# The first phase of an S4D and attention kernel, recorded and put in order by a list scheduler

## The chip, the cores and the metric

One core of one Trainium2 chip. The metric is the device time of one execution in microseconds (us); lower is better. All arithmetic is float32 (the matmuls read their operands as float32r, a float32 format of the matrix engine, and so work on high and low parts). The engines are TensorE (PE), VectorE (DVE), ScalarE (ACT), GpSimd (POOL) and SyncE (SP), whose queue issues nearly all DMA transfers.

## The reference

Two independent layers on 2048 positions of width 448, joined along the last axis:

```python
def _A_ref(u, log_A_real, A_imag, C_real, C_imag, log_dt, D_skip):
    dt = jnp.exp(log_dt)
    A = -jnp.exp(log_A_real) + 1j * A_imag
    C = (C_real + 1j * C_imag) * dt[:, None]
    P = jnp.exp((A * dt[:, None])[:, :, None] * pos[None, None, :])
    K = 2.0 * jnp.einsum("dn,dnl->dl", C, P).real       # 256 states, 2048 positions
    y = irfft(rfft(u_t, 2 * L) * rfft(K, 2 * L))[..., :L]
    return y.transpose + u * D_skip

def _B_ref(x, wqkv, wo):
    q, k, v = heads(x @ wqkv)                            # 16 heads of 28
    p = softmax(q @ k.T * 28 ** -0.5)
    return merge(p @ v) @ wo

out = concatenate([A, B], axis=-1)
```

## The kernel before

The kernel has a first phase and a main loop.

**The first phase** does two things side by side. One is the projections of attention. The input is taken in four chunks of 512 rows. A chunk is transposed on PE (`transposes`, tiles `xn`, `pt`, then `xh` and `xl`, its high and low parts), and then multiplied by the weights in 12 jobs: a key and a query job for each of four groups of four heads (`qk_proj`), and four value jobs of 128 rows (`v_proj`). That makes 48 jobs, each of 12 matmuls of up to 512 columns into one PSUM tile `pm` (three in rotation). A job's eviction writes its result as high and low part into one of two `hl` tiles (ACT, then DVE), and SP stores it to DRAM (`k`, `q`). Key jobs of the first two chunks also make differences of keys (`kb`, `dhl`, stored as `kd`, loaded again as `kdif`). Value results go through two `v` tiles.

The other is the seeds of the S4D layer: eight groups (`seeds(o)`), each a chain of 13 stages over ACT, DVE, POOL and PE. Parameters are loaded (`nat`), scaled by `dt`, transposed into PSUM (`pn`), turned into phases and sizes (`tri`, 1680 columns), through sines and exponentials on ACT (each needs its own function table, loaded on a change), multiplied on POOL and DVE, and stored as `sd` from two tiles: `se`, which shares its memory with the query tiles `qhat`, and `sg`.

Behind both come the maxima of the first unit. A unit is one group of heads with one chunk of queries. The softmax of the main loop subtracts a bound on each row, made ahead of it: 16 groups (four heads, four blocks of 128 queries) of five matmuls each against the keys `khat`, the key differences `kdif` and the negated queries `nq`, a Relu on ACT and one instruction on DVE that adds and takes the maximum. For the first unit:

```python
pd, pb = (ps_2.tile([128, 2, CQ], F32, name="p2") for _ in range(2))
kb = kt.rearrange("p (c s n) -> p c s n", c=NQ, s=2)[:, :2, 1, :]
mm(pd[:, 0], q, kd_g[0, j], start=True, stop=True)
mm(pd[:, 1], q, kt[:, 2 * CQ:3 * CQ], start=True, stop=False)
mm(pd[:, 1], nq[:, j, ts], kt[:, 3 * CQ:], start=False, stop=True)
mm(pb[:, 0].rearrange("p (c n) -> p c n", c=2), q, kb, start=True, stop=True)
mm(pb[:, 1], q, kt[:, 3 * CQ:], start=True, stop=True)
nc.scalar.activation(rl, pd, AF.Relu)
nc.vector.tensor_tensor_reduce(rl, pb, rl, 1.0, -3.0e38, ALU.add, ALU.max, m_u[0, 1][:, i:i + 1])
```

The 16 bounds of a row block are transposed (`max_end`) and written as two rows into the query tile by DMA (`max_put`), and only then can the first score matmul run (`pss<-qhat,khat`).

**What sets the order.** The phase is written as a loop over 41 steps (lines 517 to 530) that deals out projection jobs, seed stages (a new group every four steps) and loads. In this phase the entry of `KEPT` (line 88) is empty: the framework's own scheduler may reorder the instructions of each engine by its own estimates and priorities, and its result is what the profile shows. In the main loop (`KEPT["a"]`) each engine keeps the order of the program.

Two places in memory tie the order. The weights of the queries and keys lie in the tile that later takes the keys of the first group (`w_g` in `k0_t`, line 233), so a head's keys can be loaded only when the weights there are done. And in the last chunk the value jobs come first. The loads of the keys, 4 heads of 4 transfers, are asked for at steps 33, 35, 36 and 37 (`KW`, `load_k`), those of the key differences and first queries at steps 26 to 35.

**The main loop** runs over 16 units of 16 key blocks: scores, exponentials, products with the values, the next unit's maxima, and between them the S4D layer in small pieces (powers of the seeds, matmuls, Fourier steps). Its first instructions read the first unit's keys, queries, bounds, the values and the first seeds (`sdb<-sd`).

Of the kernel before, what the change touches and what calls it, by code (L numbers as in the profile page):

```python
# [8 lines left out]
F32 = mybir.dt.float32  # L9
F32R = mybir.dt.float32r  # L10
# [7 lines left out]
L = 2048  # L18
# [25 lines left out]
A0, A1, KW = 26, 34, (33, 35, 36)  # L44
# [21 lines left out]
class Kept:  # L66
# [5 lines left out]
    def __getattr__(self, name):  # L72
        f = getattr(self.engine, name)

        def call(*args, **kw):
            i = f(*args, **kw)  # L76
            return self.owner.tc.keep_in_program_order(i) if self.name in self.owner.kept else i
        return call


class Engines:
    def __init__(self, tc):
        self.tc, self.kept = tc, ()
# [8 lines left out]
def body(ctx, tc, a, out):  # L92
# [41 lines left out]
    k0_p = pool(k0_st, "k0_p", side="right")  # L134
    k0_t = k0_p.tile([128, HG, L], F32R, name="khat")
# [10 lines left out]
    def load_k(g, j, p):  # L146
        if j == 0:
            t = k0_t if g == 0 else p.tile([128, HG, L], F32R, name="khat")
# [50 lines left out]
    def max_end(u, ps):  # L199
        nc.tensor.transpose(ps[:16, :128], m_u[u, 1], ident)  # L200
        mh = q_p.tile([16, 2, 128], F32R, name="mh")
# [11 lines left out]
    with ExitStack() as st:  # L213
        sst, xst, wst, mst, psx, psm = (ExitStack() for _ in range(6))
# [3 lines left out]
        y_p = pool(wst, "y_p", side="right")  # L218
        ps_w[0] = pool(psx, "ps_w", 1, PSUM)
# [3 lines left out]

        xns = {}

        def load_x(c):
            xs = x[c * CQ:(c + 1) * CQ, :].rearrange("(t p) d -> p t d", p=128)
            for h in range(2):
                xns[c, h] = y_p.tile([128, 2, D], F32, name="xn", bufs=3)
# [6 lines left out]
        nc.gpsimd.memset(k0_t[:CK].rearrange("p g (n e) -> p (g n) e", e=32)[:, :, DH:].bitcast(F32), 0.0)  # L236
        vst = [v_p.tile([128, NK // NQ, HG, 32], F32, name="v", bufs=5).rearrange("p t h e -> p (t h) e") for _ in range(2)]
        for t in vst:
            nc.gpsimd.memset(t[:, :, DH:DH + 1], 1.0)
            nc.gpsimd.memset(t[:, :, DH + 1:], 0.0)  # L240
        wns = []
        for i in range(2):
            wn = t_p.tile([128, 3, LV, BO * 16], F32, name="tri", bufs=2).rearrange("p t k h -> p (t k h)")
            wn = wn[:CK, :2 * 3 * D].rearrange("p (k s d) -> p k s d", k=2, s=3)
            wns += [wn[:, 0], wn[:, 1]]
# [7 lines left out]
        def load_nat(o):  # L253
            nats[o] = s_p.tile([PO, 4, 256], F32, name="nat", bufs=2)
# [50 lines left out]
        def turn_dt():  # L305
            dt_ps = ps_t.tile([128, CQ], F32, name="pt")[:PO, :NO]
# [7 lines left out]
        def seeds(o):  # L314
# [13 lines left out]
            def turn():  # L328
                pn = ps_n.tile([128, CQ], F32, name="pn")
# [6 lines left out]
                q["tr"] = s_p.tile([128, NH], F32, name="tr", bufs=2)  # L336
                act.activation(q["tr"], ps[:, 0].rearrange("p b h e -> p (b h e)"), AF.Copy)

            def phases():
                tri = t_p.tile([128, 3, LV, NH], F32, name="tri", bufs=2)  # L340
# [14 lines left out]
            def places():  # L355
                se = q_p.tile([128, HG, CQ], F32R, name="qhat", bufs=3).bitcast(F32).rearrange("p h q -> p (h q)")
# [5 lines left out]
            def g_place():  # L362
                q["sg"] = sg = s_p.tile([128, BO, SDF - F_G], F32, name="sg", bufs=SGB)
# [36 lines left out]
            def g_first():  # L400

                c0 = q["ps"][:, 2:4].rearrange("p c b h e -> p c (b h e)")
                px = ps_x.tile([128, CQ], F32, name="px")
# [29 lines left out]
        def transposes(c):  # L433
            for k in range(NCK):
                pt = ps_t.tile([128, CQ], F32, name="pt")[:CK]
                for t in range(4):
                    nc.tensor.transpose(pt[:, t * 128:(t + 1) * 128], xns[c, t // 2][:, t % 2, k * CK:(k + 1) * CK], ident)
                xh[k] = x_p.tile([CK, CQ], F32R, name="xh", bufs=XB)
                xl[k] = x_p.tile([CK, CQ], F32R, name="xl", bufs=XL)
# [3 lines left out]
        def qk_proj(c, s, g):  # L443
            pp = w_tile()
# [7 lines left out]
            def evac():  # L452
                hl = x_p.tile([128, 2, CQ], F32R, name="hl", bufs=2)
# [7 lines left out]
                if s == 1 and c < 2:  # L461
                    HC = CQ // 2
                    kb = y_p.tile([128, HC], F32, name="kb")
                    dhl = y_p.tile([128, 2, HC], F32R, name="dhl")
# [10 lines left out]
        def v_proj(c, t):  # L475
            pp = w_tile()
# [12 lines left out]

        work = []  # L490
# [15 lines left out]
        pend, n_work = [], len(work)  # L506
# [7 lines left out]
        for j, t in enumerate(KW):  # L514
            ahead[t].append(lambda j=j: load_k(0, j, k0_p))

        def project():

            e = work.pop(0)() if work else None
            while pend:  # L520
                pend.pop(0)()
            if e:
                pend.append(e)

        for t in range(n_stage):
            while work and n_work - len(work) < n_work * (t + 1) / PW:
                project()
            for f in slots[t] + ahead.get(t, []):
                f()
            if t + 1 == PW:  # L530
                project()
                wst.close()
                load_k(0, HG - 1, k0_p)
                load_q(1)
                for c in range(NQ):
                    load_v(0, c)
        xst.close()
        psx.close()
        m_p = pool(mst, "m_p")
        ps_2 = pool(psm, "ps_2", 4, PSUM)  # L540
        nq = m_p.tile([128, HG, CQ], F32R, name="nq")
        m_u[0, 1] = q_p.tile([128, HG * 4], F32, name="m1", bufs=2)
        for i in range(16):
            j, t = divmod(i, 4)
            ts = slice(t * 128, (t + 1) * 128)
            q, kt = q_u[0][:, j, ts], kt_g[0][j]
            if t == 0:
                nc.gpsimd.tensor_scalar(nq[:, j], q_u[0][:, j].bitcast(F32), -1.0, None, op0=ALU.mult)
            pd, pb = (ps_2.tile([128, 2, CQ], F32, name="p2") for _ in range(2))
            kb = kt.rearrange("p (c s n) -> p c s n", c=NQ, s=2)[:, :2, 1, :]  # L550
            mm = nc.tensor.matmul
            mm(pd[:, 0], q, kd_g[0, j], start=True, stop=True)
            mm(pd[:, 1], q, kt[:, 2 * CQ:3 * CQ], start=True, stop=False)
            mm(pd[:, 1], nq[:, j, ts], kt[:, 3 * CQ:], start=False, stop=True)
            mm(pb[:, 0].rearrange("p (c n) -> p c n", c=2), q, kb, start=True, stop=True)
            mm(pb[:, 1], q, kt[:, 3 * CQ:], start=True, stop=True)
            rl = m_p.tile([128, 2, CQ], F32, name="rl2", bufs=2)
            nc.scalar.activation(rl, pd, AF.Relu)
            nc.vector.tensor_tensor_reduce(rl, pb, rl, 1.0, -3.0e38, ALU.add, ALU.max, m_u[0, 1][:, i:i + 1])
        nc.scalar.activation(half_pi[:1], half_pi[:1], AF.Exp)  # L560
        max_end(0, ps_2.tile([128, 2, CQ], F32, name="p2")[:, 0])
        max_put(0)
        psm.close()
        mst.close()
# [12 lines left out]
    k_pools = [k0_p, kq_p]  # L577
# [580 lines left out]
```

## Time and profile before

| | |
|---|---|
| median of three runs | 1304.7 us (1302.42 to 1306.85) |
| profiled execution, its own time | 1307.74 us |
| its span, first to last instruction | 1305.7 us |
| mean granted clock of TensorE | 0.976 |
| busy: PE, ACT, DVE, POOL | 94%, 75%, 69%, 66% of the span |

In a row of the profile stand the line of the kernel, the engine, the operation, the tile written and the tiles read, shapes and types. All engine calls go through one helper, so the line of nearly every instruction is that helper's call (L76 before the change, L80 or the recorder's call after it); instructions are told apart by their tiles. `p<-khat,qhat` (tile `p2`, its number left out) are the first unit's maxima, `pm<-xh,khat` and `pm<-xl,khat` are projections, because the weights lie in the tile named `khat`. `[2.18 <-DMA qhat<-mh]` behind a row means that the engine was idle for 2.18 us before it and what it waited for. SPq and ACTq are the queues in which DMAs are issued. In a table by stages, a stretch from:to in us is followed by its length, each engine's busy time and instruction count, the granted clock of PE, the busy share of the DMA engines and GB/s.

### The profile page before, as it was taken

The page shows a single profiled execution, that of the slowest core. Times are in us where ns is not written, and L with a number is a line of the kernel's source. Part 1 is how long each engine was busy: PE and PEld are TensorE (multiplying, and loading weights), DVE is VectorE, ACT ScalarE, POOL GpSimd, SP SyncE. Part 2 cuts the span into 40 slices and gives each one's busy share as a digit, 9 for nine tenths or more (in the row PEclk, how much of TensorE's full clock was granted, in tenths as well). Part 3 has the DMA queues.
Part 4 walks back from the last instruction along what each step waited for, and adds up shares of the span by engine and source line. Part 5 has one row for each costly group of instructions (what it writes and reads, how often), then busy time and mean ns, then how long its engine had stood idle before and what let it go on. Part 6 is the DMA issues. An engine that isn't in the chain of part 4 may idle for free.

```text
span 1305.7 us, 32148 instructions
## 1 busy us (share of the span) xinstructions
PE 1228.7 (94%) x12193; PEld 695.7 (53%) x12193; DVE 907.0 (69%) x2001; ACT 980.3 (75%) x2046; POOL 865.9 (66%) x684
## 2 busy tenths in 40 slices
PE   6888877799999999999999999999997999999998
PEld 5766755355555555555555555555554555545333
DVE  5676656677777787777788888888986555636111
ACT  4877875588888888888788888888886666756463
POOL 2677654478888788888769999999995221424421
PEclk9989887799999999999999999999999999999999
DMA  6677679735866455468634232743324453647666
GB/s 202 207 273 257 218 259 271 212 66 136 185 147 142 109 149 157 142 169 231 162 104 105 56 83 62 157 111 78 82 59 139 146 158 136 203 142 238 202 161 175
DMA packets 200082, 205.28 MB, mean 157 GB/s; under 512 B 95992, under 2 KB 158520, under 8 KB 197880
## 3 DMA queue, kind: packets, MB, share of 16 engines
q1 hardware_dynamic: 199864, 203.22, 56.1%
q8 instruction: 96, 1.57, 0.5%
q14 instruction: 58, 0.48, 0.1%
q10 hardware_dynamic: 64, 0.02, 0.0%
HBM read 120.74 MB, written 82.18 MB: 155 GB/s over the span
## 4 chain that ended last, share of the span: by engine, by line
PE 72%; POOL 8%; ACT 7%; DVE 5%; DMA 4%; issue 4%; SPq 0%; ACTq 0%; POOLq 0%
PE pm L76 39%; PE pss L76 16%; PE po L76 16%; POOL sg L76 2%; POOL e L76 2%; DMA khat<-k 2%; POOL tri L76 2%; ACT tri L76 1%; ACT sg L76 1%; DVE mx L76 1%; POOL p L76 1%; ACT L76 1%; ACT p L76 1%; POOL eu L76 1%; DVE rl L76 1%
## 5 line engine op out<-in xcount | busy, mean ns | idle before, releaser
L76 ACT ACTIVATE p<-pss 128x512 f32<-128x512 f32 x1024 | 560.4, 609 | 109.9 <-PE pss L76 105.9
L76 PE MATMUL pss<-qhat,khat 128*128 128x512 f32 x1024 | 405.7, 402 | 4.0 <-DMA qhat<-mh 2.2
L76 DVE TENSOR_REDUCE mx<-pm 128x1 f32<-128x512 f32 x480 | 308.3, 683 | 121.2 <-PE pm L76 119.5
L76 PE MATMUL pm<-khat,qhat 128*128 128x512 f32 x720 | 314.4, 437 | 6.1 <-ACT rl L76 3.5
L76 POOL TENSOR_TENSOR e<-e,sdb 128x256 f32<-128x256 f32 x168 | 202.0, 1203 | 108.7 <-ACT e L76 67.2
L76 PE MATMUL po<-p,v 128*32 128x512 f32 x2048 | 271.0, 597 | 0.0
L76 POOL TENSOR_TENSOR e<-e,eu 128x256 f32<-128x256 f32 x168 | 248.3, 1478 | 13.2
L76 PEld LDWEIGHTS pm<-khat,qhat 128*128 128x128 f32 x720 | 135.4, 188 | 206.4 <-ACT p L76 47.0
L76 PEld LDWEIGHTS pss<-qhat,khat 128*128 128x128 f32 x1024 | 191.2, 189 | 52.5 <-ACT p L76 13.8
L76 DVE CUSTOM_DVE_ANT_0 rl<-pm,rl 128x512 f32<-128x512 f32 x240 | 165.3, 689 | 70.0 <-ACT rl L76 67.7
L76 POOL TENSOR_TENSOR eu<-e,sdb 128x256 f32<-128x256 f32 x168 | 202.3, 1204 | 0.0
L76 POOL TENSOR_TENSOR p<-pr,pr 64x448 f32<-64x448 f32 x64 | 73.2, 1144 | 155.6 <-PE pm L76 122.3
L76 DVE TENSOR_TENSOR g<-g,zg 128x128 f32<-128x128 f32 x392 | 162.0, 413 | 3.6
L76 ACT ACTIVATE rl<-pm 128x512 f32<-128x512 f32 x240 | 145.3, 605 | 7.7 <-issue 4.1
L76 PE MATMUL pm<-xh,khat 112*128 112x512 f32 x256 | 89.7, 431 | 19.6 <-DVE hl L76 10.6
L76 PE MATMUL pm<-kdif,qhat 128*128 128x512 f32 x240 | 97.0, 404 | 1.7 <-DVE pr L76 1.1
L76 DVE TENSOR_TENSOR zg<-g,zg 128x128 f32<-128x128 f32 x224 | 88.0, 393 | 5.3
L76 PEld LDWEIGHTS pm<-e,g 128*32 128x32 f32 x3584 | 56.9, 110 | 49.2 <-issue 15.7
L76 PE MATMUL pm<-e,g 128*32 128x64 f32 x3584 | 73.6, 223 | 8.7 <-POOL e L76 8.7
L76 ACT ACTIVATE y<-pm 128x448 f32<-128x448 f32 x48 | 26.5, 553 | 59.7 <-PE pm L76 39.1
L76 PEld LDWEIGHTS pm<-xh,khat 112*128 112x128 f32 x256 | 51.0, 205 | 35.9 <-DVE hl L76 12.6
L76 DVE TENSOR_TENSOR pr<-pm,ub 128x448 f32<-128x448 f32 x64 | 37.0, 619 | 46.9 <-PE pm L76 37.7
(133 smaller groups left out, 1491.6 us busy)
## 6 DMA issues: line engine op xcount, KB each, us to landing
sdb<-sd SPq DMA_DIRECT2D x56, 336.0 KB
khat<-k SPq DMA_DIRECT2D x64, 256.0 KB
qhat<-q SPq DMA_DIRECT2D x64, 256.0 KB
sd<-sg SPq DMA_DIRECT2D x8, 1456.0 KB
k<-hl SPq DMA_DIRECT2D x16, 512.0 KB
q<-hl SPq DMA_DIRECT2D x16, 512.0 KB
v<-v SPq DMA_DIRECT2D x32, 256.0 KB
mw<-in_mw SPq DMA_DIRECT2D x16, 512.0 KB
```

What stands on the lines that cost most here:

```text
L76: i = f(*args, **kw)
```

## The change

The first phase is no longer handed to the framework in the order written. Each engine call is recorded (`Plan.add`) with its tiles and byte ranges, from which follows what each waits for (`link`). At the end `order` walks through all recorded operations with set durations, and picks at each step, for the engine that is free first, the ready operation with the longest remaining chain; the calls are then made in that order and each engine keeps it (`KEPT["p"]` names all five engines).

For this, tiles are taken in fixed rotation (`ring`) in place of pools that hand out slots. The weights get a tile of their own, `w`. Three of the four `xl` tiles lie in memory of the value tiles `v`. The first group's keys get a tile in the memory that the input tiles, the value weights `vh` and `vl`, and `kb` and `dhl` leave (`change`); they are asked for after jobs 41 to 44, the third and fourth head's first. In the last chunk the first group's key job goes ahead of the value jobs. The 16 groups of maxima are recorded from job 43 on, each in two halves of 512 columns, with two Relus and two maxima, into PSUM tiles of the projections and transposes (`pt`, `pm`); a last reduction joins the halves. Loads of the differences and first queries are asked for at steps 18 to 29 of the loop.

```diff
-A0, A1, KW = 26, 34, (33, 35, 36)
+A0, A1 = 18, 28
+MG = {41: (2, ()), 42: (3, ()), 43: (0, (8, 9)), 44: (1, (10, 11)), 45: (None, (12, 13)), 46: (None, (14, 15)), 47: (None, (0, 1)),
+      48: (None, (2, 3)), 49: (None, (4, 5)), 50: (None, (6, 7))}
...
+            if self.owner.plan is not None:
+                return self.owner.plan.add(self.name, name, f, args, kw)
...
+class Plan:
+    SPANS = {("gpsimd", "tensor_tensor", 784): 1.87, ("gpsimd", "tensor_tensor", 672): 1.73, ("gpsimd", "tensor_tensor", 1680): 3.0,
...
+             ("gpsimd", "tensor_scalar", 672): 2.28, ("gpsimd", "tensor_scalar", 512): 1.49, ("vector", "tensor_tensor", 1680): 2.3}
+    SCALE = {"p": 1.0, "s": 1.6, "m": 1.0, "d": 1.0}
+    BIAS = {"p": 0.0, "s": -20.0, "m": 0.0, "d": 0.0}
+    GAP, TABLE = 0.06, 1.28
...
+            o.span = self.SPANS.get((engine, method, n)) or {
+                "scalar": 0.2 + 0.00083 * n + (0 if tight else 0.1), "vector": 0.15 + 0.00104 * n + (0 if tight else 0.16),
+                "gpsimd": 0.2 + (0.0 if method == "memset" else 0.0025) * n}[engine]
...
+    def order(self):
...
+        for o in reversed(self.ops):
+            k = o.tag, o.engine
+            tail[o.i] = max([cost(o) + self.GAP + tail[j] for j in after[o.i]] + [o.span + chain.get(k, 0.0), cost(o)])
+            chain[k] = tail[o.i] if o.engine != "sync" else 0.0
...
+        while len(out) < n:
+            e = min((e for e in pools if pools[e]), key=lambda e: max(free[e], min(ready[i] for i in pools[e])))
+            t = max(free[e], min(ready[i] for i in pools[e]))
+            best = max((i for i in pools[e] if ready[i] <= t + 1e-9),
+                       key=lambda i: tail[i] * self.SCALE[self.ops[i].tag] + self.BIAS[self.ops[i].tag] - (0 if self.ops[i].table in (None, table[0]) else self.SWITCH))
...
-KEPT = {"p": (), "a": ("tensor", "vector", "scalar", "gpsimd", "sync"), "f": ()}
+KEPT = {"p": ("tensor", "vector", "scalar", "gpsimd", "sync"), "a": ("tensor", "vector", "scalar", "gpsimd", "sync"), "f": ()}
...
-        w_g = k0_t[:CK].rearrange("p g (i s k h e) -> p i s k g h e", i=2, s=2, k=NCK, h=HG)
+        w_t = w_p.tile([CK, HG, L], F32R, name="w")
+        w_g = w_t.rearrange("p g (i s k h e) -> p i s k g h e", i=2, s=2, k=NCK, h=HG)
...
+        def change():
+            yst.close()
+            k0.append(pool(k0_st, "k0_p", side="right"))
+            t = k0[0].tile([128, HG, L], F32R, name="khat")
+            kt_g[0] = [t[:, i] for i in range(HG)]
...
+                nc.gpsimd.tensor_scalar(Late(("nq", j), CQ, lambda: nqs[j]), q_u[0][:, j].bitcast(F32), -1.0, None, op0=ALU.mult)
...
+            for h in range(2):
+                pd, pb = pt_r(), pm_r()
+                if h == 0:
+                    mm(pd, q, kd_g[0, j], start=True, stop=True)
+                    mm(pb.rearrange("p (c n) -> p c n", c=2), q,
+                       k_late(j, CQ, lambda t_: t_.rearrange("p (c s n) -> p c s n", c=NQ, s=2)[:, :2, 1, :]), start=True, stop=True)
+                else:
+                    mm(pd, q, quarter(2), start=True, stop=False)
+                    mm(pd, Late(("nq", j), 128, lambda: nqs[j][:, ts]), quarter(3), start=False, stop=True)
+                    mm(pb, q, quarter(3), start=True, stop=True)
+                rl = rl_r()
+                nc.scalar.activation(rl, pd, AF.Relu)
+                nc.vector.tensor_tensor_reduce(rl, pb, rl, 1.0, -3.0e38, ALU.add, ALU.max, m_u[0][:, j, t, h:h + 1])
...
-            jobs = v_jobs + jobs if c == NQ - 1 else jobs + v_jobs
+            jobs = jobs[:1] + v_jobs + jobs[1:] if c == NQ - 1 else jobs + v_jobs
...
+        nc.plan = None
+        plan.run()
```

The main loop's code is the same but for the pool of the first keys, which is now made in `change`.

More of the change, by code (lines that the diff above doesn't have):

```diff
@@ L146, in load_k @@
     def load_k(g, j, p):
-        if j == 0:
-            t = k0_t if g == 0 else p.tile([128, HG, L], F32R, name="khat")
+        if g not in kt_g:
+            t = p.tile([128, HG, L], F32R, name="khat")
             kt_g[g] = [t[:, i] for i in range(HG)]
@@ L213, in body @@
     with ExitStack() as st:
-        sst, xst, wst, mst, psx, psm = (ExitStack() for _ in range(6))
+        sst, xst, wst, yst, psx = (ExitStack() for _ in range(5))
+        k0 = []
         t_p = pool(sst, "t_p")
@@ L222, in body, with ring, turn @@
         ps_x = pool(psx, "ps_x", 1, PSUM)
+        plan = nc.plan = Plan()
+        def ring(p, shape, dtype, name, n, bufs=None):
+            tiles = [p.tile(shape, dtype, name=name, bufs=bufs or n) for _ in range(n)]
+            i = [-1]
+            def turn():
+                i[0] += 1
+                return tiles[i[0] % n]
+            return turn
+        pm_r = ring(psx_p[0], [128, CQ], F32, "pm", 3)
+        pt_r = ring(ps_t, [128, CQ], F32, "pt", 2)
+        pn_r = ring(ps_n, [128, CQ], F32, "pn", 2)
+        px = ps_x.tile([128, CQ], F32, name="px")
+        xn_r = ring(y_p, [128, 2, D], F32, "xn", 3)
+        xh_r = ring(x_p, [CK, CQ], F32R, "xh", XB)
+        hl_r = ring(x_p, [128, 2, CQ], F32R, "hl", 2)
+        nat_r = ring(s_p, [128, 4, 256], F32, "nat", 2)
+        tri_r = ring(t_p, [128, 3, LV, BO * 16], F32, "tri", 2)
+        tr_r = ring(s_p, [128, BO * 16], F32, "tr", 2)
+        sg_r = ring(s_p, [128, BO, SDF - F_G], F32, "sg", SGB)
+        se_r = ring(q_p, [128, HG, CQ], F32R, "qhat", 2, 3)
+        rl_r = ring(kd_p, [128, CQ], F32, "rl", 2)
+        kb_t, dhl_t = y_p.tile([128, CQ // 2], F32, name="kb"), y_p.tile([128, 2, CQ // 2], F32R, name="dhl")
+        m_u[0], m_u[0, 1] = q_p.tile([128, HG, 4, 3], F32, name="mx", bufs=2), q_p.tile([128, HG * 4], F32, name="m1", bufs=2)
+        mh_t = q_p.tile([16, 2, 128], F32R, name="mh")
         xns = {}
@@ L240, in body @@
             nc.gpsimd.memset(t[:, :, DH + 1:], 0.0)
+        xls = [v_p.tile([128, NK // NQ, HG, 32], F32, name="v", bufs=5).rearrange("p t h e -> p (t h e)")[:CK].bitcast(F32R) for _ in range(3)]
+        xls.append(x_p.tile([CK, CQ], F32R, name="xl"))
         wns = []
         for i in range(2):
-            wn = t_p.tile([128, 3, LV, BO * 16], F32, name="tri", bufs=2).rearrange("p t k h -> p (t k h)")
+            wn = tri_r().rearrange("p t k h -> p (t k h)")
             wn = wn[:CK, :2 * 3 * D].rearrange("p (k s d) -> p k s d", k=2, s=3)
@@ L355, in places @@
             def places():
-                se = q_p.tile([128, HG, CQ], F32R, name="qhat", bufs=3).bitcast(F32).rearrange("p h q -> p (h q)")
+                se = se_r().bitcast(F32).rearrange("p h q -> p (h q)")
                 q["se"] = se = se[:, :BO * F_G].rearrange("p (b f) -> p b f", f=F_G)
@@ L452, in evac @@
             def evac():
[L453 removed]
+                hl = hl_r()
                 th, tl = hl[:, 0], hl[:, 1]
@@ L488, in v_proj @@
             return evac
+        nqs, due = {}, dict(MG)
+        groups = collections.deque([j * 4 + t for j in (2, 3, 0, 1) for t in range(4)])
+        y_all = [xn_r(), xn_r(), xn_r(), vh, vl, kb_t, dhl_t]
+        k_late = lambda j, n, f, rows=(0, 128): Late(("khat", j), n, lambda: f(kt_g[0][j]), rows)
+        def change():
[3 more added lines that the diff above has]
+            kt_g[0] = [t[:, i] for i in range(HG)]
@@ L490, in body, with first_maxima @@
+        def first_maxima(n):
+            j, ts = due.pop(n, (None, ()))
+            if j is not None:
+                first_keys(j)
+            for i in ts:
+                groups.remove(i)
+                max_group(i)
         work = []
@@ L505, in body @@
         slots[1].insert(0, turn_dt)
-        pend, n_work = [], len(work)
+        n_work = len(work)
         ahead = collections.defaultdict(list)
@@ L512, in body, with tagged @@
             ahead[A1 + i].append(lambda i=i: load_q(0, range(2 * i, 2 * i + 2)))
-        for j, t in enumerate(KW):
-            ahead[t].append(lambda j=j: load_k(0, j, k0_p))
         def project():
[L519 to L523, printed above, removed]
+            if work:
+                work.pop(0)()()
+            first_maxima(n_work - len(work))
+        def tagged(tag, f):
+            plan.tag, old = tag, plan.tag
+            f()
+            plan.tag = old
@@ L525, in body @@
         for t in range(n_stage):
             while work and n_work - len(work) < n_work * (t + 1) / PW:
-                project()
-            for f in slots[t] + ahead.get(t, []):
-                f()
-            if t + 1 == PW:
[L531 to L536, printed above, removed]
+                tagged("p", project)
+            for f in slots[t]:
+                tagged("s", f)
@@ new lines, in body @@
+            for f in ahead.get(t, []):
+                tagged("m", f)
+            if t + 1 == PW:
+                tagged("p", project)
+            elif t + 1 > PW:
+                tagged("m", lambda: first_maxima(n_work + t + 1 - PW))
+        plan.tag = "m"
+        while groups:
+            max_group(groups.popleft())
+        nc.scalar.activation(half_pi[:1], half_pi[:1], AF.Exp)
+        nc.vector.tensor_reduce(m_u[0, 1], m_u[0].rearrange("p a b c -> p (a b) c")[:, :, :2], axis=AX.X, op=ALU.max)
@@ L537, in body @@
+        max_end(0, pt_r(), mh_t)
+        max_put(0)
+        plan.do("sync", 2.0, 1 << 20, lambda: load_q(1), [], [se_r()])
+        for c in range(NQ):
+            plan.do("sync", 0.5, 1 << 18, lambda c=c: load_v(0, c), [], [(vst + xls)[c]])
+        nc.plan = None
+        plan.run()
+        wst.close()
         xst.close()
         psx.close()
[L539 to L559, printed above, removed]
```

183 lines of the change are left out of this document (154 added, 29 removed).

## The prediction

> **What bounds the kernel now.** I read the stage table first, cutting the span at the first score matmul of the main loop.
>
> ```profile
> core 0: us, PE busy (x) PEld busy (x) DVE busy (x) ACT busy (x) POOL busy (x), PEclk, DMA share, GB/s
> 7.00:200.00 193.00, 161.90 (x699) 126.86 (x697) 127.83 (x205) 142.49 (x246) 116.67 (x81) 0.93 0.72 236
> 200.00:243.00 43.00, 27.76 (x89) 17.95 (x87) 27.13 (x49) 19.48 (x25) 11.12 (x10) 0.78 1.00 277
> 243.00:1305.70 1062.70, 1037.16 (x11402) 549.53 (x11402) 751.81 (x1745) 816.91 (x1775) 735.90 (x578) 0.99 0.52 138
> ```
>
> From 243 us on TensorE (PE) is busy 1037 of 1063 us, and the diff leaves that loop alone: 1062.7 us that stay. The change works in the first 243 us, in two stages. Until 200 us (projections and seeds) no engine is full: PE 162 of 193 us, ACT 142, DMA 72%. From 200 to 243 us (the first unit's maxima) every engine idles a third or more of the time, and only DMA is full. The chain of waits says what the second stage stands on, and the timeline of PE gives its end:
>
> ```profile
> 208.44 9.86 DMA khat<-k
> 218.32 10.46 DMA khat<-k
> ...
> 236.38 5.56 DMA qhat<-mh
> ```
>
> ```profile
> 242.89 0.77 PE L76 MATMUL pss<-qhat,khat 128*128 128x512 f32 x1 [2.18 <-DMA qhat<-mh]
> ```
>
> 20.3 us of the 43 are loads of the first unit's keys: eight transfers, 2.5 us each. The last link is the write of the maxima into the queries, 5.56 us, and then the main loop begins. In the first stage the waits of ScalarE (ACT) say what the order of the work costs:
>
> ```profile
> ACT tri L76 <- POOL tri L76: 21.4, 11, 3.7
> ACT rl L76 <- PE p L76: 10.4, 11, 4.6
> ACT xh L76 <- PE pt L76: 7.0, 3, 4.9
> ACT sg L76 <- DVE px L76: 5.2, 2, 3.5
> ...
> ACT hl L76 <- DMA k<-hl: 2.4, 3, 1.4
> ```
>
> ACT idles 193 − 142.49 = 50.5 us there, 21.4 of it on GpSimd (POOL) inside the chain of one seed group, work that another group or a projection could fill.
>
> **The change part by part.** *Maxima beside projections.* In the changed program's order the 80 maxima matmuls lie among the last six of the 48 projection jobs, not behind them. What they cost on each engine comes from these rows of the groups by shape, and from one pair on ACT and three matmuls at either pace on PE:
>
> ```profile
> L76 ACT ACT_TABLE_LOAD x17 | 21.8, 1283 | 1.0 <-PEq L1148 0.7
> ...
> L76 ACT ACTIVATE rl<-p 128x1024 f32<-128x1024 f32 x16 | 16.3, 1026 | 10.9 <-PE p L76 10.4
> ...
> L76 ACT ACTIVATE rl<-pm 128x512 f32<-128x512 f32 x1 | 0.6, 598 | 4.1 <-issue 4.1
> ```
>
> ```profile
> 232.20 2.19 ACT L76 ACTIVATE rl<-p 128x1024 f32<-128x1024 f32 x2 [0.36 <-PE p L76]
> ```
>
> ```profile
> 112.62 0.63 PE L76 MATMUL pm<-xh,khat 112*128 112x512 f32 x2
> 113.09 0.40 PE L76 MATMUL pm<-xl,khat 112*128 112x512 f32 x1
> 113.33 0.63 PE L76 MATMUL pm<-xh,khat 112*128 112x512 f32 x2
> ...
> 215.11 0.63 PE L76 MATMUL p<-kdif,qhat 128*128 128x512 f32 x1
> 215.53 0.63 PE L76 MATMUL p<-khat,qhat 128*128 128x512 f32 x1
> ```
>
> PE: the count stays 80. At the fast pace (three in 113.33 − 112.62 = 0.71 us, 0.237 each) they are 19 us; at the slow pace of the maxima stage (0.42 each, granted clock 0.78 over the stage) 34 us. The changed stage mixes them with projections, so I take the fast end. ACT: each 1024-wide Relu becomes two of 512: 32 at between 0.51 us (half of 1.026) and 0.598. I take 0.58, because they queue up, as the pair in 2.19 us does, but alternate with other work: 18.6 us in place of 16.4, so +2.2. DVE gains 16 instructions of the add-and-max kind and their accumulator reads, a fraction of a microsecond each; over 243 us it is busy 155, so that hides behind its own idle time, and would cost at most the 4 or so us of their sum without it.
>
> *Table loads.* The changed order has 23 loads of ACT's tables where the old has 17: 6 × 1.283 = +7.7 us, on ACT.
>
> *The sum on ACT.* Work from 7 to 243 us: 142.49 + 19.48 − 0.60 (the one `rl` of unit 1) = 161.4; + 2.2 + 7.7 = 171.3 us. ACT takes it as the limiter: PE's fast-paced total is lower, 48 jobs × 12 × 0.237 = 137 us, transposes, and 19 us of maxima. From ACT's last Relu (232.20 + 2.19 = 234.39) to the first score matmul are 242.89 − 234.39 = 8.5 us, which I keep; the new reduction over two halves adds one small DVE instruction, and the last Relu and its max are half as long, which cancels to within 0.5 us. So the stage ends at 7 + 171.3/u + 8.5, where u is the share of time that ACT is busy. Break-even with 242.89 is at 171.3/227.4: **u = 0.75**. The old first stage has 142.49/193 = 0.74.
>
> *What raises u.* The second stage (u = 19.48/43 = 0.45) vanishes as a stage. In the first, the order by durations keeps two seed groups in flight in ACT's queue, so most of the wait on POOL (21.4) and on `px` (5.2) should find other work: I remove 18 of the 26.6 us, and the 50.5 us of idle time become 32; 171.3/(171.3 + 32) = 0.84. I take 0.85: the end at 7 + 201.5 + 8.5 = 217.0 us, 25.9 us earlier. Bounds: 0.95 if nearly every wait is filled (195.8; −47), 0.78 if only a quarter is (235.1; −8).
>
> *Keys loaded early.* Their 16 loads move up past the last query writes on SP, and the tile that takes them frees only when the last value projection is done (it reuses the space of `vh`, `vl` and the input tiles). About three quarters of ACT's work and 41 of 48 jobs precede that: 7 + 0.76 × 171.3/0.85 = 160 us. Sixteen loads at the 2.54 us of the chain take 40.6 us: the last keys are in at 201 us, and the last key set's Relus, 8 × 0.58, end at 206, beside 208.5 for ACT's own sum. So the loads are nearly co-critical; a later start counts one for one after 3 us. The bytes say the same:
>
> ```profile
> sd<-sg SPq DMA_DIRECT2D x8, 1456.0 KB
> k<-hl SPq DMA_DIRECT2D x16, 512.0 KB
> q<-hl SPq DMA_DIRECT2D x16, 512.0 KB
> sd<-qhat SPq DMA_DIRECT2D x8, 896.0 KB
> ...
> khat<-k SPq DMA_DIRECT2D x16, 256.0 KB
> ```
>
> After that point at least 16 × 256 + 7 × 512 + 2 × (1456 + 896) KB = 12.7 MB are to move, at the full stage's 277 GB/s 46 us: until 206. And the whole phase needs 0.72 × 193 + 43 = 182 us of full DMA in 217. That is tight, and it is what is late next.
>
> *Other moves.* The small key differences and the first queries are loaded among the middle chunks, where DMA has 28% free. The four negations of queries move from an idle POOL into its seed work; POOL is busy 117 of 193 us. The weights' own tile, the tiles taken in rotation and the half-tiles issue nothing.
>
> *A rule against packing.* DVE and POOL slow each other:
>
> ```profile
> 85.04 4.53 DVE L76 TENSOR_TENSOR tri<-tri 128x1680 f32<-128x1680 f32 x1
> ```
>
> ```profile
> 84.80 3.00 POOL L76 TENSOR_TENSOR tri<-tr,pw 128x1680 f32<-128x1680 f32 x1 [3.41 <-ACT tr L76]
> ```
>
> ```profile
> 185.31 1.91 DVE L76 TENSOR_TENSOR tri<-tri 128x1680 f32<-128x1680 f32 x1
> ```
>
> The same subtraction takes 1.91 us alone and 4.53 beside POOL's product, which ended at 87.80, 1.77 us before it: it waited for the whole of it. The Trainium skill (SBUF — State Buffer, "SBUF: two separate sides") says that a DVE instruction with two SBUF inputs and a POOL instruction hold the shared port pair exclusively and the other blocks. By that rule the trace agrees (4.53 − 1.91 = 2.62 us of waiting); every such pair that the tighter order lays side by side costs its overlap.
>
> **The rivals.** *Later keys, a smaller gain.* If the values finish at the old pace, 7 + 193 × 41/48 = 172 us, the loads end at 172 + 40.6 = 212.5, and Relus and tail (4.6 + 8.5) give 225.7: −17; with the loads shared with the 8.6 MB of writes, up to 10 us later still, −7. For it speaks the full DMA of the second stage; against it that ACT has fewer waits: 12%, as 1288 to 1298.
>
> *Ports.* If the eight seed groups meet all three us of a product each where one meeting cost 2.6, some 8 × 2.6 = 21 us come onto the chain that feeds ACT, less what is in the trace already (at least the one meeting): about 18, leaving −8: 1297. Against it: only waits that ACT cannot fill count. 5%. The Trainium skill's rule named above is its ground.
>
> *Everything fills.* u = 0.95: 1258. For it: all engines have room; against: DMA's 182 us. 12%, from 1256 to 1267.
>
> *Slower: evictions queue behind writes.* All five engines keep one fixed order. Five evictions `hl` of the last jobs stand in ACT's queue between groups of two to seven Relus. Each needs one of two `hl` buffers back, so waits for a 512 KB write issued on SP behind up to 15 key loads. Everything queued behind it on ACT, Relus first, waits too, and PE and DVE with them. Seven or eight loads ahead at 277 GB/s are 7.6 us, the write itself 1.9; the Relus between hide some 4 × 0.58 = 2.3. Five times 7.2 is 36 us, more than the 25.9 gained: 1315. It decides from (25.9/5) + 2.3 = 7.5 us of wait per eviction. Against it stands the row of waits of `hl` on its writes: 2.4 us in three times, longest 1.4. 11%.
>
> *Not done.* The changed order shows maxima among the projections, so this has no chance of its own.
>
> **How the numbers follow.** The profiled run has 1307.74 us with a span of 1305.7; the median is 1304.7, 3 us below it. Less 25.9 from the median: **1278.8, say 1279 us**. Chances: forecast (1267 to 1289) 60%, later keys 12%, ports 5%, everything fills 12%, evictions 11%. 0.3% (4 us) is about what a measurement can tell from no change. Some 3% of later keys and ports fall within it, hence faster 0.86, same 0.03, slower 0.11. The range reaches from u = 0.95 (1258) to u = 0.78 (1297).
>
> **What would show it.** Right: the first `pss` at 217 ± 10 us; ACT busy 83 to 87% between 7 and 208 us; PE at the fast pace in the maxima; 243 to the end unchanged at 1063 us. Wrong: a first `khat` load past 175 us, ACT waits of `hl` on writes above 7 us each, DVE's 128x1680 subtraction above 4 us in most groups, or a main loop that lengthens.

## The result, and the profile after

The changed kernel takes **1347.15 us** (median of 4 runs, 1346.68 to 1348.98), the kernel before 1304.93 us beside it (1302.42 to 1306.85): ratio **1.0327, 95% interval 1.0307 to 1.0347**. It is slower by 42 us, where 26 us faster was forecast. The profiled runs have spans of 1344.9 and 1305.7 us.

The stages of the changed kernel's span, cut at the old stage's 200 us, at the old end of the maxima, and at its own first score matmul:

```profile
core 0: us, PE busy (x) PEld busy (x) DVE busy (x) ACT busy (x) POOL busy (x), PEclk, DMA share, GB/s
7.00:200.00 193.00, 152.53 (x638) 121.20 (x636) 108.51 (x185) 139.68 (x234) 104.14 (x78) 0.86 0.67 223
200.00:243.00 43.00, 22.41 (x65) 15.46 (x64) 23.09 (x49) 19.45 (x33) 22.94 (x15) 0.68 0.70 193
243.00:287.80 44.80, 35.00 (x87) 18.31 (x85) 19.23 (x53) 15.41 (x27) 0.77 (x2) 0.76 0.54 165
287.80:1344.90 1057.10, 1034.15 (x11403) 548.36 (x11401) 752.75 (x1746) 816.61 (x1773) 735.32 (x577) 1.00 0.52 137
```

```profile
287.80 0.63 PE L80 MATMUL pss<-qhat,khat 128*128 128x512 f32 x1
```

The first score matmul comes at 287.80 us, 44.9 later than before (242.89); what follows is 5.7 shorter (1057.1 for 1062.8). In the first 200 us every engine did *less* than before (PE 152.5 us for 161.9, ACT 139.7 for 142.5, DVE 108.5 for 127.8), though the phase was meant to be packed tighter. The key loads and the maxima began late. Below, from the timelines of SP, DVE and ACT, are the first key loads, the first add-and-max and the last Relus of the first unit:

```profile
196.96 3.36 SPq L170 DMA_DIRECT2D khat<-k  x7
```

```profile
213.65 0.68 DVE L170 CUSTOM_DVE_ANT_0 rl<-pm,rl 128x512 f32<-128x512 f32 x1
```

```profile
280.92 1.21 ACT L170 ACTIVATE rl<-pt 128x512 f32<-128x512 f32 x2 [1.57 <-DVE mx L170]
```

The waits of ACT and of PE up to there, and the longest of DVE (us in total, times, longest):

```profile
ACT tri L170 <- POOL tri L170: 24.4, 11, 5.6
ACT rl L170 <- DVE mx L170: 22.7, 13, 3.5
ACT rl L170 <- PE pt L170: 11.4, 9, 3.8
```

```profile
PE pm L170 <- DVE hl L170: 18.2, 7, 8.1
PE pn L170 <- DVE tri L170: 14.7, 5, 4.4
PE pt L170 <- ACT rl L170: 11.3, 7, 7.8
```

```profile
DVE sg L170 <- POOL tri L170: 35.9, 8, 14.8
```

ACT's wait on POOL inside one seed chain, of which the forecast filled most, is still there (24.4 us; 21.4 before). New waits stand beside it: PE stands before seed transposes whose PSUM tile is not free (`pn`, 14.7 us), with the matmuls behind them, and the halves of the maxima wait for each other (22.7 + 11.4 us). The largest wait of the three engines is DVE's, on POOL in the seed chain (35.9 us; 23.2 before). So ACT, PE and DVE each stand before work that is not ready. The rows alone do not say where this begins.

**Where it comes from in the code.** `Kept.call` has two exits. With a plan it returns `plan.add(..., f, ...)`, where `f` is the engine's bare method; the line behind it, which passes the finished instruction to `tc.keep_in_program_order`, is not reached. `Plan.run` later calls `f`, and nothing ties the instruction to the one before it on its engine. So the phase is *issued* in the list scheduler's order, and the framework's scheduler may then move it: `KEPT["p"]` names five engines and acts on none of the recorded calls. That each engine keeps the planned order, as the section on the change has it, does not hold for this kernel.

### The profile page after: what moved, and what is told of

Its sections match the earlier page's. It is cut to its first block, busy times and chain, and to the rows that moved or that the text cites. A ratio compares the mean times of both kernels' runs of the same rounds, so it can differ in the third digit from the quotient of the medians.

```text
span 1344.9 us, 32229 instructions
## 1 busy us (share of the span) xinstructions
PE 1245.7 (93%) x12193; PEld 704.6 (52%) x12193; DVE 903.8 (67%) x2034; ACT 992.4 (74%) x2068; POOL 865.1 (64%) x684
## 4 chain that ended last, share of the span: by engine, by line
PE 78%; POOL 8%; DVE 5%; ACT 4%; issue 3%; DMA 1%; SPq 0%; ACTq 0%; POOLq 0%; DVEq 0%
PE pm L80 39%; PE pss L80 17%; PE po L80 16%; PE pm L170 5%; POOL sg L170 2%; POOL tri L170 2%; PE pt L170 1%; DVE mx L80 1%; POOL p L80 1%; POOL qhat L170 1%; DVE rl L170 1%; ACT p L80 1%; ACT tri L170 1%; POOL e L80 1%; ACT sg L170 1%
## 5 line engine op out<-in xcount | busy, mean ns | idle before, releaser
L170 PE MATMUL pm<-xh,w 112*128 112x512 f32 x256 | 91.7, 442 | 12.3 <-DVE hl L170 8.6
L80 PEld LDWEIGHTS po<-p,v 128*32 128x32 f32 x2048 | 54.5, 110 | 25.9 <-issue 21.4
```

What stands on the lines that cost most here:

```text
L170: f(*[x_.fn() if isinstance(x_, Late) else x_ for x_ in args], **{k: x_.fn() if isinstance(x_, Late) else x_ for k, x_ in kw.items()})
```

## The experiments

The theory, called order: the planned order is not the one that runs, and keeping it brings the forecast. The rival, called capacity: the tiles taken in rotation and the shared ports hold the packed phase back, whatever its order. All kernels compute the whole output.

| kernel | kept in order | first score matmul | rest of span | time, us |
|---|---|---|---|---|
| before | – | 242.9 | 1062.8 | 1304.9 |
| changed | none | 287.8 | 1057.1 | 1347.2 |
| pin_all | all five | 219.9 | 1058.1 | 1280.6 |
| pin_all again | all five | 222.2 | 1057.6 | 1279.8 |
| pin_no_pe | all but PE | 222.5 | 1055.7 | 1280.0 |
| pin_avp | ACT, DVE, POOL | 229.7 | 1056.6 | 1288.2 |
| pin_act_dve | ACT, DVE | 237.7 | 1056.3 | 1295.8 |
| pin_act | ACT | 259.5 | 1058.8 | 1320.1 |
| pin_pe | PE | 293.1 | 1057.5 | 1352.4 |
| written_free | none, order as written | 265.9 | 1063.8 | 1331.5 |
| written_pinned | all five, order as written | 354.9 | 1061.5 | 1418.2 |
| late_max | all five, maxima behind | 249.6 | 1056.3 | 1307.7 |
| tuned | all five, other weights | 213.8 | 1063.0 | 1277.2 |
| balanced | all five, other weights | 226.6 | 1057.3 | 1284.4 |

The changed kernel, pin_all (both times), tuned and balanced are medians of 4 or 5 runs, the other variants single runs. The kernel before, run beside each variant, had medians of 1303.0 to 1304.7. The rest of the span is the span less the start of the first score matmul, from one profiled run each.

**Keeping the planned order.**

```diff
-            f(*[...], **{...})
+            i = f(*[...], **{...})
+            if engine in PIN:
+                self.keep(i)          # tc.keep_in_program_order
+PIN = ("tensor", "vector", "scalar", "gpsimd", "sync")
```

> The changed kernel with one thing added: each recorded call, when it is made at last, is pinned behind its engine's previous instruction, as the helper does outside the recording. Theory 'order' (the recorded calls go past the pinning helper, so the framework reorders what the list scheduler had put in order, and the loss of 45 us before the first score matmul comes from that): the first pss falls from 287.8 to 205-225 us, the time to 1265-1285 us, 5% below the changed kernel. Rival 'capacity' (the loss lies in tiles in fixed rotation, maxima that share PSUM tiles with the jobs, and late keys, whatever the order): the first pss stays at 270 us or later, the time within 1330-1350 us.

Measured: **1280.61 us** (1279.82 to 1287.93), ratio to before 0.9836 (0.9805 to 0.9868). That is 66.5 us less than the changed kernel, from this edit alone. Its stages, its first score matmul, its first key loads and its waits, against the rows above:

```profile
core 0: us, PE busy (x) PEld busy (x) DVE busy (x) ACT busy (x) POOL busy (x), PEclk, DMA share, GB/s
7.00:208.00 201.00, 178.94 (x769) 136.75 (x767) 148.61 (x265) 160.16 (x277) 129.80 (x92) 0.96 0.86 276
208.00:219.90 11.90, 7.42 (x18) 3.40 (x17) 7.46 (x23) 5.30 (x10) 1.32 (x3) 0.80 0.78 274
219.90:1278.00 1058.10, 1035.11 (x11402) 549.24 (x11402) 752.37 (x1745) 816.57 (x1773) 734.85 (x576) 0.99 0.51 137
```

```profile
219.92 0.79 PE L80 MATMUL pss<-qhat,khat 128*128 128x512 f32 x1 [0.45 <-DMA qhat<-mh]
```

```profile
159.78 3.36 SPq L170 DMA_DIRECT2D khat<-k  x7
```

```profile
ACT hl L170 <- DMA k<-hl: 5.8, 4, 3.6
...
ACT rl L170 <- DVE mx L170: 4.7, 6, 1.2
...
ACT tri L170 <- POOL tri L170: 1.8, 2, 1.3
```

```profile
PE pm L170 <- DVE hl L170: 11.1, 9, 4.1
...
PE pt L170 <- ACT rl L170: 3.2, 4, 1.6
```

```profile
DVE sg L170 <- POOL tri L170: 2.0, 2, 1.8
```

ACT's wait for `mx` falls from 22.7 to 4.7 us, PE's for `pt` from 11.3 to 3.2, DVE's on POOL from 35.9 to 2.0, and ACT's on POOL's `tri` from 24.4 to 1.8: that one is filled, as the forecast had it. Tiles, ports and sizes are the same in both kernels, so the rival capacity falls. How the order differs is seen on POOL's timeline. The first key difference `dhl` runs at 21.7 us in both kernels. Kept, the second stands ahead of the first seed product, and the third between the first product and the second:

```profile
29.16 0.74 POOL L170 TENSOR_TENSOR dhl<-kb,dhl 128x256 fp32r<-128x256 f32 x1 [6.67 <-DVE hl L170]
34.70 3.00 POOL L170 TENSOR_TENSOR tri<-tr,pw 128x1680 f32<-128x1680 f32 x1 [4.81 <-ACT tr L170]
41.46 0.73 POOL L170 TENSOR_TENSOR dhl<-kb,dhl 128x256 fp32r<-128x256 f32 x1 [3.75 <-ACT dhl L170]
42.16 4.66 POOL L170 TENSOR_TENSOR tri<-tr,pw 128x1680 f32<-128x1680 f32 x1
```

In the changed kernel the two products run together, and the second and the third difference come behind them, at 36.22 and 60.42 us:

```profile
21.75 0.75 POOL L170 TENSOR_TENSOR dhl<-kb,dhl 128x256 fp32r<-128x256 f32 x1 [2.61 <-ACT dhl L170]
30.30 5.96 POOL L170 TENSOR_TENSOR tri<-tr,pw 128x1680 f32<-128x1680 f32 x2 [7.80 <-ACT tr L170]
36.22 0.73 POOL L170 TENSOR_TENSOR dhl<-kb,dhl 128x256 fp32r<-128x256 f32 x1
...
60.42 0.74 POOL L170 TENSOR_TENSOR dhl<-kb,dhl 128x256 fp32r<-128x256 f32 x1
```

**Is it one engine?** Only the list `PIN` is changed, to one engine each.

> The changed kernel with recorded calls pinned on TensorE alone. Theory 'order', with TensorE's queue as the place (transposes of seeds queued ahead of maxima and jobs wait 14.7 us on DVE's tri): first pss at 225-255 us. If the place is ScalarE or POOL, it stays above 270 us. Rival 'capacity': no change, 280-295 us.

> The changed kernel with recorded calls pinned on ScalarE alone. Theory 'order', with ScalarE's queue as the place (sines and exponentials of a seed group ahead of the Relus, 7.8 us in one wait of PE): first pss at 225-255 us. If the place is TensorE or POOL, above 270 us. Rival 'capacity': no change, 280-295 us.

PE alone brings nothing (1352.37 us, first score matmul at 293.1, so its queue alone is not the place): it then waits in a fixed order for evictions that the others still make in theirs, as its largest wait shows:

```profile
PE pm L170 <- DVE hl L170: 46.5, 13, 14.4
```

ACT alone brings 28 of the 68 us (259.5, between the two cases expected). Its wait on POOL falls to 8.5 us, while PE still waits for DVE:

```profile
ACT tri L170 <- POOL tri L170: 8.5, 4, 3.4
```

```profile
PE pm L170 <- DVE hl L170: 25.0, 11, 4.6
```

So engines were added one after the other: `PIN = ("scalar", "vector")`, then GpSimd, then SyncE.

> The planned order kept on ScalarE and VectorE alone; TensorE, GpSimd and SyncE are left free. ScalarE alone gave 1320.1 us, with TensorE still waiting 25.0 us on VectorE's evictions hl. If VectorE's late evictions are the second place where the order is lost, TensorE's waits on hl fall to near the 11.1 us of the kernel with all five kept, the first score matmul is at 220 to 235 us and the time 1281 to 1296. If GpSimd or SyncE is the second place, the gain over ScalarE alone is under 10 us: first score matmul past 250, time past 1310.

> The planned order kept on ScalarE, VectorE and GpSimd; TensorE and SyncE free. ScalarE and VectorE gave the first score matmul at 237.7 us, all five 219.9. If GpSimd's order closes the rest, it is at 217 to 226 us and the time 1278 to 1288. If it is SyncE's or TensorE's order, it stays at 232 to 243 us and the time at 1290 to 1301.

> The planned order kept on all engines but TensorE. If TensorE follows the order of its inputs by itself, the first score matmul is at 217 to 226 us and the time 1278 to 1288, as with all five. If TensorE's own order counts, above all the seed transposes that stand ahead of maxima, it is past 228 us and the time past 1289.

With DVE the first score matmul comes at 237.65 us (22 less than ACT alone; a little past the expected 235, the time within its bounds), and PE's wait on `hl` is down to near that of the kernel with all five:

```profile
PE pm L170 <- DVE hl L170: 14.4, 9, 4.1
```

GpSimd brings 8 more (229.70, between the two cases expected), SyncE 7 (222.46), and PE's own order nothing (1280.03 against 1280.61). The loss was thus spread: about 28, 22, 8 and 7 us for ACT, DVE, POOL and SP in this order of adding, one run each. The last two steps are the least certain: the first score matmul of pin_all lies 2.2 us apart in its two profiles, and its runs lie up to 8 us apart.

**Is it the keeping, or the planner's order?**

```diff
-        for i in self.order():
+        for i in range(len(self.ops)):      # order as written
```

> The changed kernel with the recorded operations called in the order in which they were written, without the list scheduler and without pins, so that the framework orders them by itself, with the new tiles, the early keys and the maxima beside projections. Theory 'order': the framework does with it about what it did with the kernel before, first pss at 235-265 us, and the step from the changed kernel shows what a list-scheduled call order does to the framework's own choice. Rival 'capacity': as slow as the changed kernel, first pss at 280-295 us, since the tiles are the same.

> All five engines keep the recorded order, but it is the order as written, without the list scheduler's times. If the planner's order is worth something beyond being kept, this one is later than its kept form (1280.6 us, first score matmul at 219.9 us): first score matmul between 230 and 260 us, time between 1291 and 1322. If merely keeping some sensible order is what counts, first score matmul within 5 us of 219.9 and time within 5 us of 1280.6. If the order as written is one that waits at the head of each engine, it is later than its free form (1331.5 us, 265.9 us).

Without keeping, the order as written gave 1331.46 us, 16 less than the planned order without keeping. Its first score matmul (265.9) is a hair past the bound expected by order, and far from capacity's. Kept, it gave **1418.15 us**, far beyond the 1291 to 1322 expected if the planner's order is better; of the three cases only the last, that it waits at the head of each engine, fits. Up to 260 us, PE stands before seed transposes whose PSUM tile `pn` DVE has not released, and before other transposes into `pt` that wait for DVE too:

```profile
PE pn L170 <- DVE pn L170: 80.1, 7, 19.2
PE pt L170 <- DVE v L170: 31.0, 4, 17.1
```

Keeping therefore costs the order as written 87 us (single runs) and saves the planned order 67: neither the order nor the keeping brings the gain by itself.

**Is it the overlap of maxima and projections?**

```diff
-MG = {41: (2, ()), 42: (3, ()), 43: (0, (8, 9)), 44: (1, (10, 11)),
...
+MG = {41: (2, ()), 42: (3, ()), 43: (0, ()), 44: (1, ())}
+        plan.floor = {o.i for o in plan.ops if o.engine == "tensor"}   # ahead of the maxima
+        if o.engine == "tensor":
+            o.before |= self.floor
```

> All five engines keep the planned order, but every maxima matmul of the first unit stands behind all the projections and seed transposes on TensorE; the keys are still loaded early. If the overlap of maxima with projections carries the gain, it is lost: with 32 Relus of 0.58 us in a stage of their own (about 19 us at best, 27 with the waits on VectorE) instead of hidden, first score matmul at 230 to 250 us, time 1291 to 1311. If the kept order by itself and the early keys carry it, first score matmul stays within 7 us of 219.9 and the time under 1288.

1307.71 us, first score matmul at 249.61: 29.7 us later than with the overlap, at the end of the expected range. The stage that the prediction saw vanish is back, with PE at a granted clock of 0.76:

```profile
200.00:249.60 49.60, 33.15 (x80) 16.66 (x81) 29.19 (x83) 24.09 (x42) 6.57 (x6) 0.76 0.56 170
```

Some 6.5 us of the 29.7 are one eviction that waits for a store, with Relus behind it on ACT:

```profile
213.52 0.60 ACT L169 ACTIVATE hl<-pm 128x512 fp32r<-128x512 f32 x1 [6.46 <-DMA q<-hl]
```

Early keys and a kept order without the overlap bring nothing over the kernel before (one run, 1303.63 beside it): the gain needs the overlap as well as the kept order. How much of the loss would be left without that one wait was not measured.

**A better order?** The kept kernel was given other weights, with which the maxima end earlier by the list scheduler's own durations.

```diff
-    SCALE = {"p": 1.0, "s": 1.6, "m": 1.0, "d": 1.0}
-    BIAS = {"p": 0.0, "s": -20.0, "m": 0.0, "d": 0.0}
-    SWITCH = 3.0
+    SCALE = {"p": 0.792, "s": 1.262, "m": 0.952, "d": 0.860}
+    BIAS = {"p": 16.74, "s": -21.82, "m": 7.13, "d": -20.5}
+    SWITCH = 11.77
```

> All five engines keep the planned order, and the list scheduler's weights (SCALE, BIAS, SWITCH) are set so that its own schedule ends its maxima 7.2 us earlier (196.3 in place of 203.5 us by its set durations), mostly by fewer changes of ScalarE's tables: SWITCH goes from 3.0 to 11.77. If the set durations are as good a model here as they were for the kernel with all five kept, the first score matmul comes at 213 us (219.9 less 7) and the time is 1273.6 us, between 1269 and 1279. If the schedule is now bound by what the durations do not show (port waits between VectorE and GpSimd, DMA times), it stays within 3 us of 1280.6.

1277.18 us (1276.19 to 1283.7, 5 runs), ratio 0.9807 (0.9783 to 0.9831). The first score matmul came as expected, but the rest of the span grew by 5 us. The timelines of PE, SP and ACT show what goes with it: the last seed group is written only at 212.37 us (204.68 in pin_all), and ACT waits for a load of seeds.

```profile
213.78 0.63 PE L80 MATMUL pss<-qhat,khat 128*128 128x512 f32 x1
```

```profile
212.37 0.36 SPq L170 DMA_DIRECT2D sd<-sg  x1
```

```profile
219.51 0.63 ACT L80 ACTIVATE e<-sdb 128x256 f32<-128x256 f32 x1 [8.47 <-DMA sdb<-sd]
```

The phase has two ends, the maxima and the seeds. Weights for both (`SCALE` 0.994, 1.495, 1.124, 0.945; `BIAS` 11.26, −16.99, 47.45, −27.71; `SWITCH` 21.13) were tried beside the kept kernel again:

> All five engines kept, with weights chosen for two ends at once: the maxima end 1.8 us earlier in the list scheduler's own schedule than with the weights as they were (201.7 in place of 203.5), and the last seed write 4.5 us earlier (198.6 in place of 203.1). In the kernel tuned for the maxima alone the first score matmul came 6.1 us earlier but ScalarE waited 8.5 us for the load of seeds sdb right behind it, and its first sixteen score matmuls took 22.1 us in place of 16.8. If the late last seed write is the cause, here the wait for sdb is gone, the first sixteen take 15 to 17.5 us, the first score matmul comes at 216 to 220 us, and the time is 1276 to 1281. If an early start of the main loop costs those 5 us by itself, the first sixteen take over 19 us.

> The same kernel as the one with all five engines kept (1280.6 us), beside the balanced one on the same chip: the time repeats within 4 us of 1280.6. The balanced kernel is 0 to 4 us faster if its schedule's gain is real, which is about what can be told apart.

Balanced: 1284.44 us (1282.37 to 1285.65), ratio 0.9851 (0.9835 to 0.9868), slower than expected. The kept kernel repeated at 1279.77, ratio 0.9821 (0.9806 to 0.9836). The wait for `sdb` is gone and the first sixteen score matmuls take 16.4 us (22.1 in tuned). But this kernel does not separate the two causes named ahead of it. Its first score matmul came at 226.62, not by 220, so it does not start early, and its last seed write (210.39) is later than pin_all's, not earlier. The table of all kernels separates them better. The rest of the span is 1061.5 to 1063.8 us in the four kernels in which ACT's first pieces wait for `sdb` (before 6.02 us, written_free 6.05, written_pinned 4.58, tuned 8.47), and 1055.7 to 1058.8 in the others, where they do not. Three of those four start late. So the longer rest goes with the wait, and not with an early start.

Why the set durations miss balanced by some 8 us is left open. One trace of it is DVE's 128x1680 subtraction, set at 2.3 us: its mean is 3.30 in balanced and 2.39 in pin_all, over eight of them 7.3 us. But in tuned, which met its forecast, it is 3.03, so this is not shown to be the reason. All three beat the kernel before, tuned by 26 us, pin_all by 23 to 24 and balanced by 19; tuned and pin_all are not told apart from each other (their intervals overlap).

## Why the prediction was wrong, by its own steps

**The step that failed** is u, the share of time in which ACT is busy, and beneath it the sentence "All five engines keep one fixed order". The prediction read `KEPT["p"]` as doing what it says, and gave the case "not done" no chance, because maxima stood among the projections. They do in the kernel that ran; but that is no proof that an order is the *planned* one. A sign stood in the prediction's own sum: the 23 table loads on ACT, which the changed kernel has, are those of the order that runs, while the planned order, kept, has 15.

**The work was sized rightly.** ACT's sum was put at 171.3 us. In the changed kernel ACT is busy 173.22 us from 7 us to the end of its last Relu (282.13; columns as in the stage tables):

```profile
7.00:282.13 275.13, 206.74 (x780) 153.27 (x778) 147.43 (x276) 173.22 (x291) 127.08 (x92) 0.82 0.67 213
```

The parts agree: 23 table loads were forecast, and 32 Relus of 0.58 us (groups by shape, to 290 us):

```profile
L170 ACT ACT_TABLE_LOAD x23 | 29.5, 1283 | 1.1 <-PEq L1379 0.7
```

```profile
L170 ACT ACTIVATE rl<-pt 128x512 f32<-128x512 f32 x32 | 18.7, 597 | 34.2 <-DVE mx L170 22.7 <-PE pt L170 11.4
```

So u is 173.2/275.1 = 0.63, not 0.85, and far below the break-even of 0.75 and the low bound of 0.78. At 0.85 the same work would have ended 71 us earlier, which is the whole miss.

**With the order kept** the forecast time is met (1280.6 against 1279; 219.9 against 217.0), but in part by luck: three terms of the sum were off and nearly cancel. To the end of its last Relu (213.60) ACT is busy 163.75 of 206.6 us:

```profile
7.00:213.60 206.60, 182.96 (x780) 138.65 (x778) 152.12 (x276) 163.75 (x283) 129.80 (x92) 0.96 0.86 279
```

So u is 0.79, not 0.85 (and the share from 7 to 208 us is 80%, not the 83 to 87 named as a sign of being right), which costs 14 us. The work is 7.5 us less, which saves 9 at the forecast's u: the planned order has 15 table loads where the prediction counted 23, 8 × 1.283 = 10.3 us fewer. From the last Relu to the first score matmul are 6.3 us, not 8.5.

```profile
L170 ACT ACT_TABLE_LOAD x15 | 19.2, 1283 | 1.0 <-PEq L1383 0.7
```

**Keys.** Forecast from 160 us: 159.78 in the kept kernel, 196.96 in the changed one, past the 175 named as a sign of error.

**Fast pace of PE in the maxima.** Right in the kept kernel: matmuls of the maxima that follow each other without a wait start 0.23 us apart (209.28, 209.51, 209.74 us), and the granted clock is 0.96 up to 208 us. Mixed in the changed one, with a granted clock of 0.68 and 0.76 in these stages: 0.23 us apart from 229.15 us, 0.43 from 239.37.

**Ports.** Not the cause. DVE's subtraction, which cost up to 4.53 us beside POOL, takes a mean of 1.94 us in the changed kernel:

```profile
L170 DVE TENSOR_TENSOR tri<-tri 128x1680 f32<-128x1680 f32 x8 | 15.6, 1944 | 0.0
```

In the kept kernel it is 2.39 us:

```profile
L170 DVE TENSOR_TENSOR tri<-tri 128x1680 f32<-128x1680 f32 x8 | 19.1, 2388 | 0.1
```

But in the kernel before it is 2.64 us:

```profile
L76 DVE TENSOR_TENSOR tri<-tri 128x1680 f32<-128x1680 f32 x8 | 21.1, 2640 | 0.1
```

So the kept order meets less of the blocking that the prediction took from the rule of the Trainium skill (SBUF — State Buffer, "SBUF: two separate sides") than the kernel before did, not more, and the changed kernel hardly any (1.94 us beside 1.91 alone). POOL is held up as well: the product at 42.16 us of the kept kernel takes 4.66 us beside DVE's subtraction (41.54 to 43.95 us), in place of 3.00. The rival's 18 us are not there.

**The rival on the slower side**, evictions behind key loads, had the right sign by the wrong mechanism: the changed kernel has no row of ACT's `hl` waiting on writes. With the order kept there are 5.8 us in four times on writes of `k`, longest 3.6, and 1.4 us in two on writes of `q`, short of the 7.5 each from which it decides.

**The main loop** was taken as unchanged. It is 5.7 us shorter in the changed kernel and 4.7 in the kept one. In the kernel before, ACT's first pieces waited for the seeds' load:

```profile
245.15 0.63 ACT L76 ACTIVATE e<-sdb 128x256 f32<-128x256 f32 x1 [6.02 <-DMA sdb<-sd]
```

In the changed and the kept kernel that wait is gone; tuned has it again (8.47), and its rest is again 1063 us.

**Two slips that changed little.** The rows of ACT's waits that the prediction put in the first stage run to 243 us; up to 200 us the waits on POOL's `tri` are 20.1 us and on `px` 3.5, so the wait to be filled was 23.6 us in place of 26.6. And a quarter of 26.6 us filled gives u = 0.80, not the low bound of 0.78.

## What to carry to other kernels

When a change puts instructions into an order, first look whether anything makes the engines keep it: follow one recorded call to the place where it is issued, and hold the sequence on one engine against the plan. Keep the engines that supply the others first: here ACT and DVE brought 50 of 68 us, and PE alone none. Price a kept order by what stands at the head of each queue, since the same keeping cost 87 us with one order and saved 67 with another. Where a phase has several ends (here maxima and seeds), look at all of them: the order tuned for one end came there 6 us earlier and gave 5 back at the other.

## What the runs showed that was not expected

Keeping PE's own order was worth nothing that these runs can tell once its suppliers kept theirs (first score matmul at 222.5 without it, 219.9 and 222.2 in two profiles with it), and keeping it alone raised its wait on `hl` from 18.2 to 46.5 us. The granted clock over the whole run was lower the longer the run took: 0.986 with the order kept, 0.958 in the changed kernel, 0.94 in the slowest variant.
